# The low halves of the first weight matrix: subtracted by VectorE in place of GpSimd

## Chip, cores and metric

One core of one Trainium2 chip. The metric is the device time of one execution in microseconds (us); smaller is better.

## What is computed

Four batches of eight heads of causal attention with a decay, and behind it two feed-forward blocks over the same 2304 tokens:

```python
scores = where(causal, -1e9, q @ k.T / 8 + cum[:, None] - cum[None, :])   # cum: running sum of log f
attn = softmax(scores); x = attn @ v                   # 4 batches, 8 heads, 576 tokens, 64 wide
h = x @ w_in; g = h * tanh(softplus(h)); z = g @ w_out # 2304 x 512 -> 2048 -> 512
m = maximum(maximum(z @ w1, z @ w2), z @ w3)           # 512 -> 768
out = m @ w_out2                                       # 768 -> 512
```

The weights arrive as 64-bit floats, so the kernel turns them into 32-bit ones itself.

## The kernel before

The matrix products of the feed-forward blocks are made of two halves. An operand t is split by `split` (L129): a high half hi in a shorter format, copied by ScalarE (L131), and a low half lo = t - hi (L137). `mm3` (L179) adds three products into PSUM: high by high (L181), high by low (L182), low by high (L183).

**First stage, where the change lies.** Two streams of work are woven together.

- Attention, sixteen pairs of heads, two units each (`scores`, L338, and `av`, L404). A score product goes to PSUM (L336). VectorE adds the decay and takes the row minimum (L390; tile mn). ScalarE does the exponential and the row sums (L396). VectorE makes the reciprocals rr (L357, L358). GpSimd scales the rows P by rr (L360). TensorE turns P (L429, tile pp), VectorE and ScalarE copy the turned blocks from PSUM into TA and TB (L433, L435), TensorE multiplies by v (L415, tile av), and the result is split into xh (ScalarE, L131) and xl (VectorE, L137). GpSimd also masks the decay tiles cb when they land (L295, L299).
- `h_steps` (L496), the first feed-forward product h = x @ w_in (L181 to L183, tile h), for blocks of 512 tokens as soon as attention has finished them; the results he are copied from PSUM (L522, L519) and sent to DRAM.

`load_w_in` (L198) brings w_in in sixteen pieces of 128 x 512 values: a load by SyncE's queue (L146, tile wr), then `convert` (L151): absolute value by ScalarE (L156), clamp by GpSimd (L160), shift and two merges of the words by VectorE (L163, L166, L170, tile wt), then `split`: high half by ScalarE (L131, tile wi), low half by GpSimd (L137, tile wi). There are two wt buffers, so the absolute value of a piece waits until the subtraction two pieces before has read its buffer.

The order on each engine is made by a scheduler that simulates the program with priorities: attention stands under a high priority (L537), `wgen` (the weight pieces) and the h steps are advanced in between at a fixed rate (L543, L550). An engine works off its instructions strictly in that order.

**Later stages**: h times w_out with the Mish function between, then the three maxima, then the output product. Their code is not touched.

Of the kernel before, what the change touches and what calls it, by code (L numbers as in the profile page):

```python
# [64 lines left out]
def tile_decay_attention__mish_ff__max3_ff(  # L65
# [63 lines left out]
    def split(dst_hi, dst_lo, src, eng_hi, eng_lo):  # L129
        if eng_hi == "act":  # L130
            nc.scalar.activation(dst_hi, src, AF.Copy)  # L131
        elif eng_hi == "pool":
            nc.gpsimd.tensor_scalar(dst_hi, src, 1.0, 1.0, op0=ALU.mult, op1=ALU.mult)
        else:
            nc.vector.tensor_copy(dst_hi, src)
        eng = nc.gpsimd if eng_lo == "pool" else nc.vector
        return eng.tensor_tensor(out=dst_lo, in0=src, in1=dst_hi, op=ALU.subtract)  # L137
# [3 lines left out]
    def fetch(pool, src, bufs):  # L141

        m, n = src.shape[0] // 128, src.shape[1]
        r = pool.tile([128, m, n, 2], I32, name="wr", tag="wr", bufs=bufs)
        with queued(pace):
            nc.sync.dma_start(  # L146
                r.rearrange("p m n w -> p m (n w)"), src.bitcast(I32).rearrange("(m p) w -> p m w", p=128)
            )
        return r

    def convert(pool, r, bufs=None, abs_eng="dve"):  # L151

        t = pool.tile([128, r.shape[1], r.shape[2]], F32, name="wt", tag="wt", bufs=bufs)
        lo, hi, ti = r[:, :, :, 0], r[:, :, :, 1], t.bitcast(I32)
        if abs_eng == "act":
            nc.scalar.activation(t, hi.bitcast(F32), AF.Abs)  # L156
        else:
            nc.vector.tensor_scalar(ti, hi, 0x7FFFFFFF, None, op0=ALU.bitwise_and)
        eng = nc.gpsimd if abs_eng == "act" else nc.vector
        eng.tensor_scalar(  # L160
            t, t, F32_MIN_AS_HIGH_HALF, F32_MAX_AS_HIGH_HALF, op0=ALU.max, op1=ALU.min
        )
        nc.vector.tensor_scalar(  # L163
            ti, ti, 3, 0x3FFFFFF8, op0=ALU.logical_shift_left, op1=ALU.bitwise_and
        )
        nc.vector.scalar_tensor_tensor(  # L166
            out=ti, in0=hi, scalar=-0x40000000, in1=ti,
            op0=ALU.bitwise_and, op1=ALU.bitwise_or,
        )
        nc.vector.scalar_tensor_tensor(  # L170
            out=ti, in0=lo, scalar=29, in1=ti,
            op0=ALU.logical_shift_right, op1=ALU.bitwise_or,
        )
        return t
# [20 lines left out]
    wi = [wpool.tile([128, 2, KD, 256], F32R, name=f"wi{fp}") for fp in range(NFP)]  # L195
    loaded = set()

    def load_w_in():  # L198
        jobs = [(fp, c) for fp in range(NFP) for c in range(0, KD, 2)]
        raws = []  # L200
        for k, (fp, c) in enumerate(jobs):
            for f_, c_ in jobs[len(raws):k + 3]:
                raws.append(fetch(wst, moe_w_in[c_ * 128:(c_ + 2) * 128, f_ * 256:f_ * 256 + 256], 4))
            if k == 0:
                yield
            t = convert(wst, raws[k], abs_eng="act")
            split(wi[fp][:, 0, c:c + 2], wi[fp][:, 1, c:c + 2], t, "act", "pool")
            if c + 2 == KD:
                loaded.add(fp)
            yield  # L210
# [285 lines left out]
    def h_steps():  # L496
# [3 lines left out]
        for i, j in order:  # L500
# [28 lines left out]
            yield i  # L529

    wgen = load_w_in()
    attn = attention()
    steps = h_steps()
# [294 lines left out]
    for t0 in (BLK2, BLK2 + 2 * HALF):  # L828
        hh = [hp2.tile([128, 2 * HALF], F32R, name=f"hh{c}") for c in range(NF2)]
        hl = [hp2.tile([128, 2 * HALF], F32R, name=f"hl{c}") for c in range(NF2)]  # L830
        for p in range(3):
            fs = slice(p * 128, p * 128 + 128)
            for m in range(3):
                S = []
                for k in range(4):
                    t = sst.tile([128, 2, 2, 128], F32R, name="s")
# [88 lines left out]
```

## Time and profile before

| | |
|---|---|
| median of 3 runs | 910.57 us (909.36 to 911.1) |
| the profiled execution | 909.78 us, of it 907.7 us span |
| TensorE (PE) busy | 882.8 us, 97% of the span |
| VectorE (DVE) busy | 497.1 us, 55% |
| ScalarE (ACT) busy | 400.7 us, 44% |
| GpSimd (POOL) busy | 232.7 us, 26% |
| loads and stores | 145.25 MB, mean 160 GB/s |

The span is what the profiler saw between the first and the last instruction; the execution's own time is 2.1 us longer. Shares are means over stages with different limits, so what is to be read is the stage in which the change lies, the first 160 us.

### The profile page before, as it was taken

The numbers are of one execution on the slowest core, as the hardware profiler recorded it, in microseconds if no ns is written. First come the engines' busy times: TensorE is split into PE (matmuls) and PEld (weight loads), VectorE is DVE, ScalarE is ACT, GpSimd is POOL, SyncE is SP. The second block draws the span as 40 slices with busy tenths as digits, with TensorE's granted clock in tenths as the row PEclk, the third lists the DMA queues.
The fourth block names the chain that finished last, engine by engine and source line by source line (L and its number), as shares of the span: only waits on it lengthen the run. The fifth ranks groups of instructions, "written<-read, shape, count | busy, mean of one in ns | idle before, by whom it ended". The sixth has DMA issues, their size and how long they took to land.

```text
span 907.7 us, 13930 instructions
## 1 busy us (share of the span) xinstructions
PE 882.8 (97%) x4800; PEld 704.8 (78%) x4800; DVE 497.1 (55%) x1186; ACT 400.7 (44%) x913; POOL 232.7 (26%) x317
## 2 busy tenths in 40 slices
PE   6898999999999999999999999999999999999998
PEld 3565666767767778889888888889888998889986
DVE  3598675344444343991367575775855447424440
ACT  4687666454443432533465545553433222412211
POOL 3689987222222220000020000000121332013310
PEclk8989999999999999999999999999999999999999
DMA  7896664444333115863456666663499444333401
GB/s 183 227 226 171 179 192 117 115 134 127 105 102 108 47 48 178 292 226 128 143 181 217 214 216 222 217 226 98 162 359 322 124 123 117 111 96 126 139 23 60
DMA packets 125030, 145.25 MB, mean 160 GB/s; under 512 B 64736, under 2 KB 78048, under 8 KB 124960
## 3 DMA queue, kind: packets, MB, share of 16 engines
q1 hardware_dynamic: 105856, 102.41, 39.0%
q10 hardware_dynamic: 16416, 27.79, 8.3%
q0 software_dynamic: 2688, 14.16, 4.3%
q8 instruction: 38, 0.62, 0.3%
q14 instruction: 32, 0.26, 0.1%
HBM read 102.83 MB, written 41.49 MB: 159 GB/s over the span
## 4 chain that ended last, share of the span: by engine, by line
PE 89%; POOL 3%; DMA 2%; DVE 2%; issue 1%; ACT 1%; SPq 1%; POOLq 0%
PE y L181 7%; PE y L183 7%; PE y L182 7%; PE h L181 7%; PE h L182 7%; PE h L183 7%; PE q L182 6%; PE q L183 6%; PE q L181 6%; PE sc L336 5%; PE av L415 5%; PE pp L429 5%; PE o L181 3%; PE o L182 3%; PE o L183 3%; PE g L181 2%
## 5 line engine op out<-in xcount | busy, mean ns | idle before, releaser
L181 PE MATMUL h<-xh,wi 128*128 128x512 f32 (+1 forms) x320 | 121.4, 380 | 1.6 <-ACT he L522 1.3
L182 PE MATMUL h<-xl,wi 128*128 128x512 f32 (+1 forms) x320 | 120.6, 377 | 1.8 <-DVE xl L137 1.8
L183 PE MATMUL h<-xh,wi 128*128 128x512 f32 (+1 forms) x320 | 120.7, 377 | 0.0
L182 PE MATMUL y<-gl,wo 128*128 128x512 f32 (+1 forms) x320 | 117.7, 368 | 0.0
L183 PE MATMUL y<-gh,wo 128*128 128x512 f32 (+1 forms) x320 | 117.6, 368 | 0.0
L181 PE MATMUL y<-gh,wo 128*128 128x512 f32 (+1 forms) x320 | 106.3, 368 | 0.0
L360 POOL TENSOR_SCALAR P<-P,rr 128x128 f32<-128x128 f32 (+3 forms) x128 | 74.0, 592 | 87.5 <-DVE rr L358 31.5
L659 DVE TENSOR_TENSOR gl<-g,gh 128x512 fp32r<-128x512 f32 x72 | 50.0, 697 | 83.3 <-ACT gh L658 83.1
L396 ACT ACTIVATE P<-P,mn 128x128 f32<-128x128 f32 (+3 forms) x128 | 70.7, 554 | 53.4 <-DVE mn L390 50.2
L652 ACT ACTIVATE g<-g 128x512 f32<-128x512 f32 x72 | 45.2, 632 | 70.6 <-DMA g<-h_d 65.7
L181 PEld LDWEIGHTS h<-xh,wi 128*128 128x128 f32 x320 | 60.1, 188 | 14.6 <-issue 2.2
L182 PEld LDWEIGHTS h<-xl,wi 128*128 128x128 f32 x320 | 60.1, 188 | 14.0 <-issue 2.8
L183 PEld LDWEIGHTS h<-xh,wi 128*128 128x128 f32 x320 | 60.3, 188 | 11.5 <-issue 2.7
L182 PEld LDWEIGHTS y<-gl,wo 128*128 128x128 f32 x320 | 60.3, 188 | 10.2
L183 PEld LDWEIGHTS y<-gh,wo 128*128 128x128 f32 x320 | 60.2, 188 | 10.1
L181 PEld LDWEIGHTS y<-gh,wo 128*128 128x128 f32 x320 | 60.3, 189 | 10.1
L522 ACT ACTIVATE he<-h 128x512 f32<-128x512 f32 x56 | 33.3, 595 | 57.0 <-PE h L183 52.4
L851 DVE TENSOR_TENSOR u<-q,p 128x448 f32<-128x448 f32 x36 | 22.4, 621 | 62.3 <-PE q L183 60.7
L336 PE MATMUL sc<-kT,qT 64*128 64x128 f32 (+3 forms) x256 | 51.9, 500 | 3.6 <-DVE mn L390 3.3
L429 PE MATMUL pp<-ident,P 128*128 128x128 f32 x320 | 51.1, 285 | 4.0 <-ACT qT L314 3.6
L658 ACT ACTIVATE gh<-g 128x512 fp32r<-128x512 f32 x72 | 45.0, 627 | 22.0 <-PE y L183 20.9
L429 PEld LDWEIGHTS pp<-ident,P 128*128 128x128 f32 x320 | 37.0, 143 | 20.1 <-issue 5.0
(141 smaller groups left out, 1850.3 us busy)
## 6 DMA issues: line engine op xcount, KB each, us to landing
g<-h_d SPq DMA_DIRECT2D x72, 256.0 KB, 2.9
s<-s_d SPq DMA_DIRECT2D x72, 256.0 KB, 3.0
h_d<-he ACTq DMA_DIRECT2D x56, 256.0 KB, 2.9
wr<-in_moe_w_out_dram SPq DMA_DIRECT2D x22, 512.0 KB, 4.6
wr<-in_moe_w_dram SPq DMA_DIRECT2D x24, 384.0 KB, 3.8
s_d<-sk POOLq DMA_DIRECT2D x12, 768.0 KB, 5.8
cb<-cum_d SPq DMA_DIRECT2D x32, 256.0 KB, 4.2
wr<-in_moe_w_in_dram SPq DMA_DIRECT2D x16, 512.0 KB, 4.5
```

The costliest lines, as they stand in the source:

```text
L181: nc.tensor.matmul(ps, wh, xh, start=start, stop=False, skip_group_check=True)
L182: nc.tensor.matmul(ps, wh, xl, start=False, stop=False, skip_group_check=True)
L183: return nc.tensor.matmul(ps, wl, xh, start=False, stop=stop, skip_group_check=True)
L336: nc.tensor.matmul(dst, lhs, J["k"][rows, c0:c0 + w], start=True, stop=True, skip_group_check=True)
L360: nc.gpsimd.tensor_scalar(made[ci], made[ci], rr[:, ci:ci + 1], 1.0, op0=ALU.mult, op1=ALU.mult)
L396: nc.scalar.activation(Pt, Pt, AF.Exp, scale=-1.0, bias=mn[:, col - 1:col], accum_out=sm[:, ci:ci + 1],)
L415: last = nc.tensor.matmul(acc[(U, L)[h], off:off + w], J["vs"][:, n * 64:n * 64 + 64], T[:, at[h]:at[h] + w], start=kt == 0 and off == 0, ...
L429: turn = nc.tensor.transpose(pp[:, n * 128:n * 128 + 128], Pt[:, k0:k0 + 128], ident)
L522: nc.scalar.activation(he, h, AF.Copy)
L652: nc.scalar.activation(g, g, AF.Mish)
L658: on_act[:] = [nc.scalar.activation(gh, g, AF.Copy)]
L659: on_dve[:] = [nc.vector.tensor_tensor(out=gl, in0=g, in1=gh, op=ALU.subtract)]
```

## The change

One word: the engine of the low half's subtraction of w_in goes from GpSimd to VectorE. The clamp (L160) and the scaling of P (L360) stay on GpSimd. Sixteen subtractions of 128 x 512 values are concerned.

```diff
@@ load_w_in @@
             t = convert(wst, raws[k], abs_eng="act")
-            split(wi[fp][:, 0, c:c + 2], wi[fp][:, 1, c:c + 2], t, "act", "pool")
+            split(wi[fp][:, 0, c:c + 2], wi[fp][:, 1, c:c + 2], t, "act", "dve")
```

The scheduler makes a new order with it on every engine, from about 50 us to the end of attention.

On GpSimd, at the fourth and fifth pieces of w_in, between two scalings of P of one unit (L360). L295 masks the decay tiles of a later pair.

```order
 L360 TENSOR_SCALAR P_0_1143<-P_0_1143,rr 128x384
 L360 TENSOR_SCALAR P_1_1149<-P_1_1149,rr 128x384
-L137 TENSOR_TENSOR wi_149<-wt,wi_149 128x512
-L160 TENSOR_SCALAR wt<-wt 128x512
-L295 AFFINE_SELECT cb<-cb 128x2x256
-L137 TENSOR_TENSOR wi_150<-wt,wi_150 128x512
-L295 AFFINE_SELECT cb<-cb 128x2x128 x2
+L160 TENSOR_SCALAR wt<-wt 128x512
+L295 AFFINE_SELECT cb<-cb 128x2x256
+L295 AFFINE_SELECT cb<-cb 128x2x128 x2
+L160 TENSOR_SCALAR wt<-wt 128x512
 L360 TENSOR_SCALAR P_0_1156<-P_0_1156,rr 128x512
 L360 TENSOR_SCALAR P_1_1162<-P_1_1162,rr 128x512
```

Both subtractions are gone, and the clamp of the next piece has moved up, ahead of the scaling of the wide P.

On VectorE, the place where the second piece is converted, before:

```order
L390 ISA P_None,mn<-sc,cb_602 128x288
L390 ISA mn 128x1
L358 RECIPROCAL rr<-rr 128x2
L390 ISA P_None,mn<-sc,cb_602,mn 128x288
L390 ISA mn 128x1
L163 TENSOR_SCALAR wt<-wt 128x512
L166 SCALAR_TENSOR_TENSOR wt<-wr,wt 128x512
```

and now:

```order
L390 ISA P_None,mn<-sc,cb_602 128x288
L390 ISA mn 128x1
L163 TENSOR_SCALAR wt<-wt 128x512
L137 TENSOR_TENSOR wi_148<-wt,wi_148 128x512
L358 RECIPROCAL rr<-rr 128x2
L390 ISA P_None,mn<-sc,cb_602,mn 128x288
L390 ISA mn 128x1
L166 SCALAR_TENSOR_TENSOR wt<-wr,wt 128x512
```

The shift L163, which waits for GpSimd's clamp, and the moved subtraction, which waits for ScalarE's high half, now stand ahead of a reciprocal and of the second half of a row minimum.

On VectorE again, ahead of the subtraction that gives xl for an h step. Before:

```order
L170 SCALAR_TENSOR_TENSOR wt<-wr,wt 128x512
L390 ISA P_None,mn<-sc,cb_819 128x288
L390 ISA mn 128x1
L137 TENSOR_TENSOR xl_447<-av,xh_446 128x256
L433 COPY TB<-pp 128x512
```

and now:

```order
L390 ISA P_1_1293,mn<-sc,cb 128x256
L390 ISA mn 128x1
L137 TENSOR_TENSOR wi_150<-wt,wi_150 128x512
L163 TENSOR_SCALAR wt<-wt 128x512
L433 COPY TB<-pp 128x512
L137 TENSOR_TENSOR xl_447<-av,xh_446 128x256
```

The same xl comes four row minima later in the order, behind a moved subtraction, a shift and a copy.

## Rows read from the trace of the kernel before

**Rows 1.** The page: busy us (share of span) xinstructions; POOL in 40 slices, tenths.
```profile
PE 882.8 (97%) x4800; PEld 704.8 (78%) x4800; DVE 497.1 (55%) x1186; ACT 400.7 (44%) x913; POOL 232.7 (26%) x317
...
POOL 3689987222222220000020000000121332013310
```

**Rows 2.** Windows: stretch, its length, busy us (xcount) by engine, PEclk, DMA share, GB/s.
```profile
48.00:160.00 112.00, 104.60 (x714) 72.73 (x713) 84.64 (x243) 75.05 (x208) 97.18 (x108) 0.98 0.65 176
60.00:100.00 40.00, 36.50 (x270) 25.53 (x270) 33.26 (x91) 27.81 (x78) 37.55 (x43) 1.00 0.75 195
...
160.00:440.00 280.00, 280.00 (x1712) 214.18 (x1710) 133.91 (x389) 121.95 (x309) 47.64 (x92) 1.00 0.42 133
```

**Rows 3.** Timeline of PE: start, duration, instruction, count [idle before <-releaser].
```profile
45.38 1.11 PE L429 MATMUL pp<-ident,P 128*128 128x128 f32 x4 [3.61 <-ACT qT L314]
...
79.79 0.50 PE L182 MATMUL h<-xl,wi 128*128 128x512 f32 x1 [1.80 <-DVE xl L137]
...
85.13 0.92 PE L336 MATMUL sc<-kT,qT 64*128 64x384 f32 x4 [1.25 <-DVE mn L390]
...
106.83 0.88 PE L336 MATMUL sc<-kT,qT 64*128 64x384 f32 x2 [2.00 <-DVE mn L390]
...
145.97 0.50 PE L181 MATMUL h<-xh,wi 128*128 128x512 f32 x1 [1.32 <-ACT he L522]
```

**Rows 4.** Windows of 2 us behind the long wait; the third number from the end is PEclk.
```profile
46.00:48.00 2.00, 2.00 (x11) 1.03 (x9) 1.82 (x6) 2.00 (x7) 1.91 (x2) 0.50 1.24 226
48.00:50.00 2.00, 2.00 (x12) 1.99 (x11) 2.00 (x9) 1.44 (x6) 0.62 (x2) 0.50 0.83 184
50.00:52.00 2.00, 2.00 (x7) 0.73 (x6) 2.00 (x9) 1.94 (x8) 1.32 (x2) 0.51 1.02 266
```

**Rows 5.** Timeline of DVE at the waits of PE.
```profile
77.31 1.71 DVE L170 SCALAR_TENSOR_TENSOR wt<-wr,wt 128x512 int32<-128x512 int32 x1
...
79.32 0.41 DVE L137 TENSOR_TENSOR xl<-av,xh 128x256 fp32r<-128x256 f32 x1
...
81.99 1.23 DVE L357 TENSOR_SCALAR rr<-sums 128x3 f32<-128x3 f32 x1
...
102.95 0.43 DVE L163 TENSOR_SCALAR wt<-wt 128x512 int32<-128x512 int32 x1 [2.50 <-POOL wt L160]
```

**Rows 6.** Timeline of POOL at the same places.
```profile
77.21 1.26 POOL L137 TENSOR_TENSOR wi<-wt,wi 128x512 fp32r<-128x512 f32 x1
...
81.76 1.43 POOL L137 TENSOR_TENSOR wi<-wt,wi 128x512 fp32r<-128x512 f32 x1
...
98.72 2.30 POOL L295 TENSOR_SCALAR_AFFINE_SELECT cb<-cb 128x512 f32<-128x512 f32 x3 [0.93 <-DMA cb<-cum_d]
101.01 1.91 POOL L160 TENSOR_SCALAR wt<-wt 128x512 f32<-128x512 f32 x1
```

**Rows 7.** Tile wt, 40 to 160 us: duration ns min/median/max, first and last start us.
```profile
L160 POOL TENSOR_SCALAR wt<-wt x16: 1904/1916/2091, 43.2 to 140.2; 128x512 f32<-128x512 f32 x16
L163 DVE TENSOR_SCALAR wt<-wt x16: 417/427/1508, 45.2 to 142.4; 128x512 int32<-128x512 int32 x16
...
L170 DVE SCALAR_TENSOR_TENSOR wt<-wr,wt x16: 678/740/1709, 48.6 to 143.8; 128x512 int32<-128x512 int32 x16
L131 ACT ACTIVATE wi<-wt x16: 615/630/636, 50.0 to 144.8; 128x512 fp32r<-128x512 f32 x16
```

**Rows 8.** Lines of POOL and of DVE, 48 to 160 us: busy, mean | idle before, releasers.
```profile
L137 POOL TENSOR_TENSOR wi<-wt,wi 128x512 fp32r<-128x512 f32 x16 | 22.1, 1391 | 2.1 <-ACT wi L131 2.1
...
L163 DVE TENSOR_SCALAR wt<-wt 128x512 int32<-128x512 int32 x15 | 8.8, 586 | 14.4 <-POOL wt L160 14.4
```

**Rows 9.** Instructions of lines 357, 659 and 137 on DVE: duration ns min/median/max.
```profile
L357 DVE TENSOR_SCALAR rr<-sums x64: 147/170/1374, 17.0 to 337.6; 128x2 f32<-128x2 f32 x48, 128x3 f32<-128x3 f32 x16
...
L659 DVE TENSOR_TENSOR gl<-g,gh x72: 678/693/953, 423.3 to 622.4; 128x512 fp32r<-128x512 f32 x72
...
L137 DVE TENSOR_TENSOR xl<-av,xh x48: 197/380/426, 28.7 to 356.0; 128x256 fp32r<-128x256 f32 x24, 128x64 fp32r<-128x64 f32 x8, 128x192 fp32r<-128x192 f32 x8, 128x128 fp32r<-128x128 f32 x8
```

**Rows 10.** Timeline of ACT ahead of the last wait of PE.
```profile
144.80 0.63 ACT L131 ACTIVATE wi<-wt 128x512 fp32r<-128x512 f32 x1 [1.63 <-DVE wt L170]
```

## The prediction

> **What bounds the kernel now.** I read the page first: TensorE is busy for 97% of the span, GpSimd for 26%, but its slices show it at nine tenths only between the third and the seventh, that is up to about 160 us [rows 1]. So the share of the whole says nothing, and I went to the windows. From 160 to 440 us TensorE is busy in 280.00 of 280 us: nothing that another engine does there could make it faster, and a time saved or lost earlier is passed on to the end unchanged. From 48 to 160 us TensorE is busy in 104.60 of 112 us, GpSimd in 97.18, VectorE in 84.64 [rows 2]. All sixteen moved subtractions lie in this stretch. **What the change can give is therefore at most the 7.4 us that TensorE stands idle there** (112 - 104.60), and the question is which of it hangs on GpSimd.
>
> Then the timeline of TensorE. Four waits make 6.37 us of the 7.4: 1.80 us for an xl, 1.25 and 2.00 us for row minima, 1.32 us for ScalarE's copy he [rows 3]. A fifth, 3.61 us at 45.38 us, comes ahead of the first moved instruction and stays as it is; so does the half clock that follows it, 0.50 in the three windows from 46 to 52 us [rows 3, 4].
>
> Then the engines that were waited for. Ahead of the xl at 79.32 us VectorE's merge L170 took 1.71 us, where its shortest takes 0.68; it began at 77.31, a tenth of a us after GpSimd's subtraction at 77.21, which ran until 78.47. Ahead of the row minima at 84 us the little L357 took 1.23 us instead of 0.15; it began at 81.99, and GpSimd's subtraction of 81.76 ran until 83.19 [rows 5, 6, 7, 9]. In both, VectorE's instruction ends its usual length after GpSimd's subtraction has ended: it was **held**. Five such holds by a subtraction of w_in stand in the timeline (the others at 69, 127 and 134 us), about 1.05 us each. The xl subtraction, which reads PSUM and one tile of SBUF, shows none of it: 0.38 us in the median, 0.43 at the longest [rows 9].
>
> The Trainium skill has the reason on its page "SBUF — State Buffer", section "Who interferes with whom": VectorE and GpSimd share one pair of SBUF ports, taken as a lock for a whole instruction, by any GpSimd operation and by VectorE's two-port modes or operations with two SBUF inputs. The rows agree (held from start to end, 1.71 against 0.68 us). The rule also speaks against this change, since the moved subtraction has two SBUF inputs wherever it runs; that is the third rival below.
>
> **The change, part by part.** The sum is made against the profiled execution, 909.78 us, which lies 0.79 us under the median of 910.57; I add that at the end.
>
> 1. *Removed from GpSimd*: 16 subtractions, 22.1 us in the stretch [rows 8]. GpSimd goes from 97.18 to about 75.1 of 112 us, from 87% to 67%. It stops being the fullest engine after TensorE.
> 2. *The hold ahead of the xl*: 1.71 - 0.68 = 1.03 us of the 1.80 us wait goes. The rest of that wait (0.77) is the merge and the row minimum that stand ahead of xl, and they remain.
> 3. *The hold ahead of the row minima*: 1.23 - 0.15 = 1.08 of 1.25 us goes.
> 4. *The 2.00 us wait at 106.83*: VectorE stood 2.50 us for a clamp [rows 5], and that clamp stood in GpSimd's queue behind masks, which had themselves waited 0.93 us for a load [rows 6]. So the subtractions are only part of the lateness. Bounds 0 and 2.00; nothing divides it better, so I take the middle, 1.0.
> 5. *The 1.32 us wait at 145.97*: ScalarE stood 1.63 us for a merge of w_in, with he queued behind its high half [rows 10]; the merge was late because its clamp was. Bounds 0 and 1.32; I take the middle, 0.66.
> 6. *Added to VectorE*: 16 subtractions. The nearest row is gl, the same shape and formats on this engine: 0.69 us, up to 0.95 [rows 9]. 16 x 0.69 = 11.0 us; the five holds give back 5 x 1.05 = 5.3. VectorE goes from 84.64 to about 90.4 of 112 us, 81%. I cost it at nothing on the path: VectorE stands 14.4 us waiting for clamps in this stretch [rows 8], and an emptier GpSimd makes those earlier, so the new work fills idle time. If that cover is gone the price is that of the first rival.
> 7. *New waits*: the subtraction waits on VectorE for ScalarE's high half, and the order puts row minima, reciprocals (which GpSimd's scaling waits for) and the xl behind it. On GpSimd the same wait cost 2.1 us in all [rows 8]; below lies nothing, and above all sixteen times a whole high half, 16 x 0.63 = 10.1 us [rows 7]. The order leaves other work between a piece's last merge and its subtraction, so I stay with the nearest row, 0 to 2.1, on an engine with slack: nothing on the path.
> 8. *A new order on TensorE*: the kinds of product change 378 times in the old order and 375 times in the new. No term.
> 9. *Loads*: the same loads in a new order on SyncE's queue; TensorE waited for none in this stretch. No term.
>
> Sum: 1.03 + 1.08 + 1.0 + 0.66 = 3.77 us less. 909.78 - 3.8 = 906.0, and with 0.79 for the median **906.8 us**. What is late next is VectorE itself, which then carries more than GpSimd.
>
> **The rivals.** A measurement of this kernel tells a change from none at about 0.2%, 1.8 us.
>
> - *VectorE fills up (slower).* From 60 to 100 us VectorE is busy in 33.26 of 40 us [rows 2], and some 6.4 of the sixteen pieces fall there (16 x 40/100). Its idle 6.74 us pay 1.05 us for each: **over 1.05 us per subtraction, held time and waits for ScalarE included, VectorE becomes the bound**. A subtraction that meets a clamp in the middle takes 0.69 + 1.92/2 = 1.65 us; 6.4 x 1.65 = 10.6, or 3.8 us too much, which TensorE loses behind xl and the row minima. 909.78 + 3.8 + 0.79 = 914.4 us. For it: shifts and merges of w_in already stretch to 1.5 and 1.7 us [rows 7], and the order puts the shift, which waits for the clamp, ahead of a row minimum. Against it: half of what stretches them disappears, and 14.4 us of waiting for the clamp is there to be used. One more wait of TensorE as long as 3.61 us could also bring a second stretch at half clock, some 3 us more [rows 3, 4]. Chance 0.20.
> - *The order swallows it (no change).* The scheduler made a different order on every engine for 100 us; other places become late in place of these, as the xl that now stands behind a moved subtraction. Then 910.6 us. Nothing in the profile speaks for it except that each of the four waits is under 2 us and has its own cause. Chance 0.10.
> - *The hold changes sides (no change).* The subtraction is held by clamps and holds GpSimd in turn; its 11.0 us take the place of 22.1, so half of the holds come back. Terms 4 and 5 then give nothing, 2 and 3 give half: 2.11/2 = 1.06, and 910.57 - 1.06 = 909.5 us. For it: L170, the merge with the same two SBUF inputs, was held for 1.03 us by GpSimd. Against it: on VectorE the subtraction is half as long as on GpSimd (0.69 against 1.39 us), so it is in the way for a shorter time. By the Trainium skill's section named above the port lock would do exactly this. Chance 0.15.
>
> **How the numbers follow.** Forecast, faster by over 0.2%: 0.55. No change, the second and third rival: 0.25. Slower: 0.20. The best case is that all 7.4 us of idle time go: 909.78 - 7.4 + 0.79 = 903.2 us, the low end. The high end is the price of the first rival, 914.4 us; beyond it lies about half of that rival's 0.20 (several subtractions held for a whole clamp, or a second stretch at half clock), so some 0.1 is left out there and little below. The forecast's own range is 903.2 to 908.7.
>
> **What would show it.** Right: in the same stretch (up to 160 us) GpSimd falls by about 22 us of busy time, VectorE rises by 5 to 7, TensorE's idle time behind 48 us falls from 7.4 to about 3.6; the sixteen subtractions of wi stand on VectorE with a median near 0.7 us; L357 and L163 have few instructions over 1 us; VectorE's wait for the clamp falls well under 14.4 us; from 160 us on nothing differs but a shift. Wrong: a median of the wi subtraction over 1.05 us, new waits of TensorE for xl or mn of 2 us and more, or a TensorE clock under 1.00 between 60 and 160 us.

## The result, and the profile after

| | before | after |
|---|---|---|
| median of 5 runs | 910.46 us (909.36 to 911.1) | **915.59 us** (915.05 to 919.91) |
| the profiled execution | 909.78 us, span 907.7 | 915.05 us, span 913.2 |

The ratio is 1.0072, with a 95% interval of 1.0046 to 1.0098: slower by 0.7%, where 906.8 us was forecast.

The page of the changed kernel: busy time by engine, and GpSimd's slices.

```profile
PE 885.9 (97%) x4800; PEld 707.8 (78%) x4800; DVE 499.7 (55%) x1202; ACT 401.4 (44%) x913; POOL 214.4 (23%) x301
...
POOL 3689763222222220000010000000121323013310
```

And the windows of the same three stretches.

```profile
48.00:160.00 112.00, 101.68 (x668) 68.21 (x666) 85.07 (x255) 73.20 (x200) 78.50 (x91) 0.97 0.60 167
60.00:100.00 40.00, 34.73 (x249) 22.75 (x247) 35.66 (x108) 29.71 (x84) 35.63 (x39) 0.96 0.70 190
160.00:440.00 280.00, 279.73 (x1728) 216.00 (x1728) 134.28 (x390) 121.72 (x310) 47.80 (x92) 1.00 0.43 134
```

Beside [rows 2]: from 48 to 160 us GpSimd fell by 18.7 us (97.18 to 78.50) and VectorE rose by 0.4, although it has sixteen subtractions more (over the whole span by 2.6, 497.1 to 499.7; at 160 us the changed kernel is behind and has done less of its other work). So the work went where it was meant to go, and yet TensorE's idle time in the stretch rose from 7.4 to 10.3 us. From 160 to 440 us TensorE is full, as before.

The span grew by 5.5 us: 2.4 are more idle time of TensorE (24.9 to 27.3 over the whole span), 3.1 more busy time for the same 4800 products. Most of both comes from two places of the stretch. The timeline of TensorE there:

```profile
80.70 0.55 PE L429 MATMUL pp<-ident,P_None 128*128 128x128 f32 x3 [1.88 <-DVE TB L433]
82.53 0.99 PE L429 MATMUL pp<-ident,P 128*128 128x128 f32 x4 [1.29 <-ACT TB L435]
...
126.10 0.50 PE L181 MATMUL h<-xh,wi 128*128 128x512 f32 x1 [2.94 <-ACT he L522]
```

None of the four waits of [rows 3] is left; these three stand ahead of other products. Behind each of the two places the granted clock fell from 1.00 (2.4 GHz) to 0.50 (1.2 GHz) for some 3.4 us. Windows of 2 us, PEclk third from the end:

```profile
82.00:84.00 2.00, 1.47 (x6) 1.13 (x8) 2.00 (x7) 2.00 (x9) 2.00 (x3) 0.66 0.71 218
84.00:86.00 2.00, 2.00 (x6) 0.72 (x3) 2.00 (x8) 1.45 (x5) 1.91 (x4) 0.50 0.81 199
126.00:128.00 2.00, 1.90 (x7) 1.42 (x8) 1.87 (x6) 1.67 (x6) 1.55 (x3) 0.76 0.71 246
128.00:130.00 2.00, 2.00 (x8) 1.36 (x7) 1.94 (x4) 1.79 (x5) 2.00 (x2) 0.50 0.77 187
130.00:132.00 2.00, 2.00 (x9) 1.08 (x8) 0.74 (x1) 0.79 (x2) 1.91 (x3) 0.89 0.20 71
```

A window at share c does (1 - c) of its length less work, so by this estimate the two spells cost 1.7 us each. The first spell, at 46 us, was shorter in this execution (0.78, 0.50 and 0.87 from 44 to 50 us) than in the one of before [rows 4], which gives 1.7 back. Of the 3.1 us more busy time that leaves 1.4 that I can't place.

What was late at these places stands on VectorE:

```profile
77.48 0.84 DVE L163 TENSOR_SCALAR wt<-wt 128x512 int32<-128x512 int32 x1 [1.37 <-POOL wt L160]
78.25 0.90 DVE L137 TENSOR_TENSOR wi<-wt,wi 128x512 fp32r<-128x512 f32 x1
79.07 0.90 DVE L166 SCALAR_TENSOR_TENSOR wt<-wr,wt 128x512 int32<-128x512 int32 x1
...
79.97 0.68 DVE L433 COPY TB<-pp 128x512 f32<-128x512 f32 x1
...
123.54 0.62 DVE L163 TENSOR_SCALAR wt<-wt 128x512 int32<-128x512 int32 x1 [2.67 <-POOL wt L160]
124.09 0.50 DVE L390 CUSTOM_DVE_ANT_0 P_None<-sc,cb,mn 128x288 f32<-128x288 f32 x1
```

Both times the shift L163 stands at VectorE's head and waits for GpSimd's clamp, 1.37 and 2.67 us, and what TensorE needs is queued behind it: at 79.97 the copy TB, at 124.09 the second half of a row minimum. Ahead of the copy the moved subtraction itself adds 0.90 us. The second one goes on through ScalarE, where the exponential waited 3.48 us for that minimum, with the copy he of the h step behind it:

```profile
124.70 0.78 ACT L396 ACTIVATE P_None<-P_None,mn 128x576 f32<-128x576 f32 x1 [3.48 <-DVE mn L390]
...
125.47 0.58 ACT L522 ACTIVATE he<-h 128x512 f32<-128x512 f32 x1
```

The moved operation itself did what was forecast. The steps of one piece (tile wt), with durations in ns min/median/max:

```profile
L160 POOL TENSOR_SCALAR wt<-wt x16: 1907/1917/2234, 43.1 to 130.6; 128x512 f32<-128x512 f32 x16
L163 DVE TENSOR_SCALAR wt<-wt x16: 398/427/843, 45.0 to 132.9; 128x512 int32<-128x512 int32 x16
...
L170 DVE SCALAR_TENSOR_TENSOR wt<-wr,wt x16: 667/692/1085, 48.1 to 134.5; 128x512 int32<-128x512 int32 x16
...
L137 DVE TENSOR_TENSOR wi<-wt,wi x16: 672/716/1037, 52.0 to 136.9; 128x512 fp32r<-128x512 f32 x16
```

Against [rows 7] the longest shift fell from 1508 to 843 ns and the longest merge from 1709 to 1085: the holds by GpSimd's subtraction are gone. In return some of GpSimd's instructions are held by the moved subtraction. What is left on GpSimd took 3.4 us more than before (78.50 against 97.18 - 22.1 = 75.1), and the longest scaling of P rose from 1.17 to 1.64 us; it began while a subtraction ran on VectorE:

```profile
127.00 1.02 DVE L137 TENSOR_TENSOR wi<-wt,wi 128x512 fp32r<-128x512 f32 x1
...
127.47 1.64 POOL L360 TENSOR_SCALAR P<-P,rr 128x512 f32<-128x512 f32 x1
```

The last clamp starts at 130.6 us instead of 140.2: the pieces come earlier, and TensorE gained nothing by it.

So two things changed at once, the engine of an operation and the scheduler's order on all engines. The experiments take them apart.

### The profile page after: what moved, and what is told of

Same layout as the page of the kernel before. It is cut to its first block, busy times and chain, and to the rows that moved or that the text cites. A ratio compares the mean times of both kernels' runs of the same rounds, so it can differ in the third digit from the quotient of the medians.

```text
span 913.2 us, 13993 instructions
## 1 busy us (share of the span) xinstructions
PE 885.9 (97%) x4800; PEld 707.8 (78%) x4800; DVE 499.7 (55%) x1202; ACT 401.4 (44%) x913; POOL 214.4 (23%) x301
## 4 chain that ended last, share of the span: by engine, by line
PE 87%; DVE 4%; DMA 3%; POOL 2%; issue 1%; ACT 1%; SPq 1%; POOLq 0%; ACTq 0%
PE y L181 7%; PE y L183 7%; PE y L182 7%; PE h L181 7%; PE h L183 6%; PE h L182 6%; PE q L182 6%; PE q L181 6%; PE q L183 6%; PE sc L336 5%; PE pp L429 5%; PE av L415 4%; PE o L181 3%; PE o L182 3%; PE o L183 3%; PE g L181 2%
## 5 line engine op out<-in xcount | busy, mean ns | idle before, releaser
L360 POOL TENSOR_SCALAR P<-P,rr 128x128 f32<-128x128 f32 (+3 forms) x128 | 75.3, 603 | 102.6 <-DVE rr L358 59.2
L658 ACT ACTIVATE gh<-g 128x512 fp32r<-128x512 f32 x72 | 44.9, 626 | 19.6 <-PE y L183 18.7
```

The source lines that it names most:

```text
L360: nc.gpsimd.tensor_scalar(made[ci], made[ci], rr[:, ci:ci + 1], 1.0, op0=ALU.mult, op1=ALU.mult)
L658: on_act[:] = [nc.scalar.activation(gh, g, AF.Copy)]
```

## The experiments

Where an order is "held", a table of instruction numbers gives each engine's order in the first stage, and a call at the kernel's end adds an order-only dependency between neighbours on each engine. In the traces of runs 1, 2, 4, 7 and 11 every instruction that was not moved stands in the order of the table from the first piece on. No run holds an order without any other edit, so what the call costs by itself is not measured. The call:

```diff
         tile_decay_attention__mish_ff__max3_ff(tc, *args)
+        pinned(nc, tc)
```

All results, each with its own ratio to the kernel before on the same chip (median of before 909.7 to 910.5 us):

| run | subtraction, clamp | order | median us | ratio (95%) |
|---|---|---|---|---|
| 1 | DVE, POOL | before's, held | 907.42 | 0.9972 (0.9962 to 0.9983) |
| 2 | POOL, POOL | changed one's, held | 929.54 | 1.0207 (1.0192 to 1.0222) |
| 3 | DVE, POOL | changed one's, three moved | 917.67 | 1.0086 (1.0066 to 1.0105) |
| 4 | DVE, DVE | changed one's, held | 906.54 | 0.9965 (0.9952 to 0.9978) |
| 5 | DVE, POOL | pieces later | 910.26 | 1.0009 (0.9995 to 1.0023) |
| 6 | DVE, POOL | pieces earlier | 913.67 | 1.0044 (1.0030 to 1.0059) |
| 7 | DVE, DVE | before's, held | **901.37** | 0.9910 (0.9897 to 0.9924) |
| 8 | DVE, DVE | its own | 905.90 | 0.9964 (0.9951 to 0.9977) |
| 9 | DVE, DVE | pieces earlier | 910.56 | 1.0004 (0.9994 to 1.0014) |
| 10 | DVE, DVE | pieces later | 909.18 | 0.9989 (0.9978 to 0.9999) |
| 11 | POOL, DVE | before's, held | 903.15 | 0.9916 (0.9902 to 0.9929) |
| 12 | POOL, DVE | its own | 915.52 | 1.0062 (1.0048 to 1.0075) |
| 13 | POOL, POOL | another from 89 us on (rate 0.98) | 912.72 | 1.0033 (1.0021 to 1.0045) |
| 14 | POOL, POOL | before's again (rate 1.05) | 909.73 | 0.9998 (0.9989 to 1.0007) |
| 15 | DVE, POOL | changed one's again to 361 us (rate 0.98) | 921.50 | 1.0110 (1.0083 to 1.0137) |
| 16 | DVE, POOL | changed one's again to 180 us (rate 1.05) | 919.39 | 1.0092 (1.0074 to 1.0110) |

**Runs 1 and 2: the engine and the order apart.** My theory: the loss is the order's. The rival: VectorE with the subtractions is what makes TensorE wait.

Run 1 is the changed kernel with the table of before's order (the subtractions stand where the scheduler likes them); run 2 the kernel before with the table of the changed order.

> The sixteen subtractions run on VectorE as in the change, but every other instruction of every engine is held to the order of the kernel before by edges between neighbours; only where on VectorE the subtractions stand is left to the scheduler. Theory 1, the loss comes from the new order (VectorE stands in its queue for GpSimd's clamp ahead of attention's work, and two waits of TensorE of about 3 us end in a stretch at half clock): the loss goes away, 906 to 911 us, with no half clock between 60 and 160 us and TensorE idle for under 7.4 us from 48 to 160. Theory 2, the loss is the 11 us of work that VectorE has more: still 914 us or more.

> The counterpart: the sixteen subtractions stay on GpSimd as in the kernel before, but every other instruction is held to the order that the scheduler made for the change. Theory 1 (order): as slow as the change or slower, 915 to 922 us, since the clamps come later still behind the subtractions. Theory 2 (VectorE's load): back near 910.5 us.

Run 1, the window of 48 to 160 us:

```profile
48.00:160.00 112.00, 106.86 (x728) 74.68 (x727) 84.70 (x261) 77.00 (x215) 79.00 (x92) 0.98 0.65 176
```

Run 1 took 907.42 us, under both kernels. VectorE and GpSimd are as busy as in the changed kernel (84.70 and 79.00 against 85.07 and 78.50), and TensorE stands idle for 5.1 us where it stood for 10.3. **The move of the subtraction alone gives about 2.5 us; the new order costs some 8** (915.59 against 907.42). Against the expectation one spell at half clock is left between 60 and 160 us, 0.57 in the two windows from 106 to 110. Run 2 says the same from the other side: without the move, the new order costs 19 us, more than the 915 to 922 us that I had expected. There GpSimd has the subtractions again, and through the two wt buffers ScalarE waits for them, from 40 to 160 us:

```profile
ACT wt L156 <- POOL wi L137: 35.9, 12, 5.3
```

(us in total, times, longest). The absolute value of a piece waits for a free buffer with exponentials queued behind it. What is left in run 1 above 1 us is one wait; timelines of TensorE, VectorE and GpSimd:

```profile
104.27 0.88 PE L336 MATMUL sc<-kT,qT 64*128 64x384 f32 x2 [2.44 <-DVE mn L390]
```

```profile
99.83 0.43 DVE L163 TENSOR_SCALAR wt<-wt 128x512 int32<-128x512 int32 x1 [3.85 <-POOL wt L160]
```

```profile
95.84 0.64 POOL L295 TENSOR_SCALAR_AFFINE_SELECT cb<-cb 128x512 f32<-128x512 f32 x1 [3.24 <-DMA cb<-cum_d]
...
97.88 1.92 POOL L160 TENSOR_SCALAR wt<-wt 128x512 f32<-128x512 f32 x1
```

The clamp stands in GpSimd's queue behind masks that wait for a load. It is the wait of 2.00 us in [rows 3], with the same cause as in [rows 6], not shortened by the move.

**Run 3: is it the three places?** The changed order with three instructions moved: on VectorE the copy TB ahead of the shift L163, and the second half of a row minimum ahead of the later L163; on ScalarE another TB ahead of an absolute value L156. The two on VectorE:

```diff
+L433 COPY TB<-pp 128x512
 L163 TENSOR_SCALAR wt<-wt 128x512
 L137 TENSOR_TENSOR wi_150<-wt,wi_150 128x512
 L166 SCALAR_TENSOR_TENSOR wt<-wr,wt 128x512
 L357 TENSOR_SCALAR rr<-sums_172 128x3
-L433 COPY TB<-pp 128x512
...
-L163 TENSOR_SCALAR wt<-wt 128x512
 L390 ISA P_None,mn<-sc,cb_1238,mn 128x288
 L390 ISA mn 128x1
+L163 TENSOR_SCALAR wt<-wt 128x512
```

> The changed kernel with its own order held, but for three instructions: on VectorE the copy TB that TensorE waited for at 80.7 us is put ahead of the shift that waits for a clamp; on ScalarE the copy TB that it waited for at 82.5 us is put ahead of an absolute value; on VectorE the second half of the row minimum is put ahead of the shift that stood 2.67 us for a clamp, which made TensorE wait 2.94 us at 126.1. Theory 1 (these waits, and the half clock behind them): most of 1.88 + 1.29 + 2.94 = 6.1 us of waits goes and so do the two stretches of 3.4 us at half clock, in all 5 to 8 us less, 907.5 to 911 us. Theory 2 (load): the waits turn up elsewhere, 914 us or more.

The first theory fell: 917.67 us. The three waits went and two others came, for a row minimum (2.7 us) and for a copy by ScalarE (2.9 us). From TensorE's waits from 40 to 160 us, in total, times, longest:

```profile
PE sc L336 <- DVE mn L390: 4.1, 4, 2.7
...
PE pp L429 <- ACT q L317: 2.9, 1, 2.9
```

Each was again followed by a spell at half clock (84 to 88 and 128 to 136 us). I read the three places as symptoms: with them mended, TensorE waits elsewhere in the same order.

**Runs 4, 7, 8, 11, 12: the clamp.** The clamp goes to VectorE too, so that no step of VectorE waits for GpSimd in the middle of a piece; in runs 11 and 12 it goes alone.

```diff
-        eng = nc.gpsimd if abs_eng == "act" else nc.vector
+        eng = nc.vector
```

> The changed kernel in its own order, but the sixteen clamps also run on VectorE (0.36 to 0.42 us each, 6 to 7 us more work there, about 31 us less on GpSimd). Where they stand on VectorE is left to the scheduler. Theory 1, VectorE stands 13.6 us for clamps that are late on GpSimd and that is what makes TensorE wait: those waits go to zero, 906 to 912 us although VectorE works more. Theory 2, VectorE has too much work: slower than the change, 917 us or more.

> The subtraction and the clamp on VectorE, everything else in the order of before. If waiting for GpSimd's clamp is what is left of TensorE's waits (2.44 us for a row minimum and the half clock behind it in the run with the old order): 903.5 to 905.5 us, TensorE busy in over 108 of 112 us from 48 to 160 us. If VectorE's own load (then some 90 of 112 us) is what is left: 906 to 908 us, as with the clamp on GpSimd. Between this and the run with the clamp on VectorE in the changed order (906.54 us) stands what the two orders cost when nothing waits for GpSimd: nothing, if the order hurts only through the clamp; up to 8 us, if it hurts by itself.

> The subtraction and the clamp on VectorE, in the order that the scheduler makes for that, with nothing held fixed. If a fresh order costs only where pieces wait for GpSimd in between: 904 to 908 us. If each fresh order is a draw, good or bad by some us: anything from 904 to 916 us, and outside 904 to 908 it speaks for the draw.

> The kernel before, in its own order held fixed, with the clamp alone moved to VectorE; the subtraction stays on GpSimd. If the two moves add up: before 909.7, less the 6.0 us that the clamp's move gave behind the subtraction's (907.42 to 901.37): 903.7 us. If GpSimd's subtractions still hold VectorE's merges and make TensorE wait for xl and row minima: 906 to 909 us, with L170 or L357 over 1.2 us at the longest.

> The same edit in the order that the scheduler makes for it, nothing held. If a fresh order costs some us wherever it comes from: 906 to 914 us, over the run with the order fixed by 2 us or more. If it does so only where VectorE waits for GpSimd's clamp: as the run with the order fixed, within 2 us.

In the changed order the clamp's move brings 9 us (915.59 to 906.54), in before's order 6 behind the subtraction's (907.42 to 901.37, 2 us better than the most I had expected) and 7 alone. Windows of runs 4, 7, 11 and 12, in this order:

```profile
48.00:160.00 112.00, 107.61 (x720) 72.54 (x717) 88.96 (x278) 77.70 (x216) 53.27 (x78) 0.98 0.63 173
60.00:100.00 40.00, 36.65 (x252) 23.93 (x253) 39.14 (x123) 31.29 (x88) 24.98 (x36) 0.96 0.79 212
```

```profile
48.00:160.00 112.00, 110.14 (x759) 77.02 (x758) 93.40 (x281) 80.31 (x222) 51.51 (x78) 1.00 0.68 182
60.00:100.00 40.00, 38.89 (x287) 27.21 (x286) 38.51 (x114) 29.11 (x81) 21.78 (x32) 1.00 0.81 212
```

```profile
48.00:160.00 112.00, 110.20 (x742) 76.55 (x743) 89.76 (x264) 79.03 (x218) 68.32 (x94) 0.98 0.68 181
```

```profile
48.00:160.00 112.00, 98.72 (x665) 67.10 (x665) 85.16 (x252) 73.22 (x199) 67.81 (x92) 0.96 0.60 166
```

VectorE is busy for 39.14 and 38.51 of 40 us in runs 4 and 7, far more than in the changed kernel (35.66), and both are faster: a full VectorE is not the bound. What fits all these runs is a VectorE that *stands* ahead of attention's work. In run 7 no wait of TensorE in the stretch is longer than 0.8 us, and its median is the lowest of all, 0.9% under the kernel before; run 11, whose interval overlaps with its own, is not clearly behind. Run 8, both moves in a fresh order, took 905.90 us, 4.5 more than run 7; that lies inside both of its ranges and decides nothing.

Run 11 has the subtraction on GpSimd, and the holds with it:

```profile
L170 DVE SCALAR_TENSOR_TENSOR wt<-wr,wt x16: 680/872/1656, 48.4 to 136.9; 128x512 int32<-128x512 int32 x16
```

The longest merge still takes 1.66 us, and no wait for xl or a row minimum is among TensorE's from 40 to 160 us (of my rival there came the holds, not the time). So in before's order, with the clamp gone from GpSimd, the holds cost TensorE nothing. That they made it wait in [rows 3] because waits for the clamp had used up the slack is my reading; no run shows it by itself.

Runs 11 and 12 are the same edit in two orders, 903.15 and 915.52 us, 12 us apart, more than any engine move here is worth (what this one brings in before's order is 7). In run 12 the shift no longer waits for a clamp, yet TensorE waits 10.7 us for row minima (six times, longest 4.7), because the chain now goes through the buffers:

```profile
ACT wt L156 <- POOL wi L137: 12.3, 8, 2.9
```

```profile
92.57 0.46 DVE L160 TENSOR_SCALAR wt<-wt 128x512 f32<-128x512 f32 x1 [1.78 <-ACT wt L156]
...
94.66 0.68 DVE L390 CUSTOM_DVE_ANT_1 P<-sc,cb 128x512 f32<-128x512 f32 x1
```

It is the same figure with another instruction in it: a step of w_in stands ahead of a row minimum and waits. That a fresh order costs only where VectorE waits for GpSimd's clamp falls with run 12, which is also 1.5 us slower than the other range that I had given.

**Runs 5, 6, 9, 10: the places of the pieces.** The order is cut in two: the 128 instructions of w_in's pieces, and all others. Runs 5 and 10 take the others from the changed order and the pieces' places from before's, runs 6 and 9 the reverse, held by the same call. Places don't carry over exactly, and both overshoot: shifts stand behind 58.7 row minima in the mean (5, 10) and 53.0 (6, 9).

> The subtraction on VectorE. Attention and the h steps stand in the changed kernel's order among themselves; the sixteen pieces of w_in (loads, absolute value, clamp, shift, merges, halves) are put back to where the order of before has them, by the count of other instructions ahead of them in the whole program, which puts the sixteen shifts 58.7 row minima from the start in the mean (changed kernel 55.0, before 56.8). If the changed kernel is slow because its pieces stand too early, ahead of clamps that are not ready (my theory now): 906 to 909 us, no half clock between 60 and 160 us. If the order of attention itself is the worse one: 914 to 917 us, as the changed kernel, with waits for sc or pp of 2 us and more in about the same places.

> The counterpart. The subtraction on VectorE, attention and the h steps in the order of before, the pieces of w_in put to where the changed kernel has them, by the same count; that makes them stand earlier still (53.0 row minima ahead of a shift in the mean, against 55.0). If pieces that stand too early are the cause: 914 to 920 us, with VectorE's wait for the clamp over 13.6 us and a half clock between 60 and 160 us. If the order of attention is the cause: 906 to 909 us, as with everything in the order of before (907.4).

> As the run with the pieces earlier in the order of before (913.67 us), and the clamp on VectorE too. If pieces that stand too early hurt only because VectorE then waits for GpSimd's clamp: 901 to 903 us, as with the pieces in their old places (901.37). If they hurt by themselves (ScalarE's halves and absolute values and VectorE's work ahead of attention): 905 to 910 us, with waits of TensorE for xh, xl or mn of over 1 us between 60 and 110 us.

> As the run with the pieces later in the changed kernel's attention order (910.26 us), and the clamp on VectorE too. The changed order with the clamp on VectorE took 906.54 us, the order of before 901.37: of these 5.2 us either the places of the pieces are the cause, then this takes 901 to 903.5 us, or attention's own order, then 905 to 907 us.

With the clamp on GpSimd the four corners are 907.42 (both from before), 913.67 (pieces earlier), 910.26 (attention from the changed one) and 915.59 us (both). By these medians the places of the pieces carry 5.3 to 6.3 us of the 8.2, attention's own order 1.9 to 2.8. Runs 5 and 6 lie between the two ranges given for each, and the changed order itself took up to 921.50 us in runs 15 and 16 below, so the sizes, and which of the two carries more, are not settled. The expected side effect did not come: in run 6 VectorE waits only 4.8 us for the clamp, but 5.5 us in nine waits for the high half wi; which link of a piece is the late one changes with the order. With the clamp on VectorE the corners are 901.37, 910.56, 909.18 and 906.54: earlier pieces cost 9.2 us in before's order and nothing in the changed one (906.54 against 909.18). Run 10 is slower than either of its ranges. "Too early" is therefore no property of the pieces alone, and that pieces hurt only through the clamp is refuted by run 9.

**Runs 13 to 16: other orders of both kernels?** Only the rate at which h steps are advanced is changed, which was to make the scheduler order all engines anew.

```diff
-        credit += RATE
+        credit += 0.98 * RATE
```

> The kernel before; only the rate at which h steps are advanced beside attention is 0.98 of what it was, which makes the scheduler draw another order on every engine and moves no work between engines. If before's order is not special: 909 to 911.5 us. If it is a good draw among many: slower by 3 us or more, 913 to 922 us.

> The same with the rate at 1.05, whose order is nearer to that of before. Not special: 909 to 911.5 us; a good draw: 912 us or more.

> The changed kernel (subtraction on VectorE), with the rate at 0.98. If the loss belongs to the move: 914 to 917 us, as the changed kernel. If the order is a draw: anywhere from 905 to 925 us, and a difference of over 3 us from 915.6 speaks for the draw.

> The changed kernel with the rate at 1.05. If the loss belongs to the move: 914 to 917 us. If the order is a draw: anywhere from 905 to 925 us, and a difference of over 3 us from 915.6 speaks for the draw.

Three of the four are no other orders. In the trace of run 14 every engine has the same instructions in the same sequence as in the kernel before, to the end. In runs 15 and 16 every engine has the changed kernel's sequence up to 361 and 180 us, so in the whole stretch, and TensorE waits in the same places, as its waits of run 15 show:

```profile
PE h L181 <- ACT he L522: 3.6, 1, 3.6
PE pp L429 <- DVE TB L433: 1.9, 1, 1.9
```

So these three are repeats. Run 14 repeats the kernel before within 0.1%. Runs 15 and 16 repeat the loss, and with the same order in the stretch they are 3.8 to 5.9 us slower than the changed kernel (run 15 alone spans 914.15 to 923.15 us). Part of that is the clock: 0.94 from 48 to 160 us in both against 0.97. My bound for a draw, over 3 us from 915.6, was passed without another order and so shows no draw; nor does run 3, 2.1 us over the changed kernel in nearly the same order, differ from it clearly.

Only run 13 is another order: 912.72 us, 2.2 more than the kernel before, between its two ranges. Of the subtraction alone on VectorE no second order of the stretch was measured, so whether the scheduler's orders for this edit are all bad stays open. What is shown is that the loss is not in the engine move, which gains in before's order.

## Why the prediction was wrong

- **Terms 1 and 6 held in the main.** GpSimd fell by 18.7 us (22.1 forecast), since 3.4 us came back as holds on its other instructions. VectorE rose by 0.4 (5 to 7 forecast), since more was given back than the five holds of 1.05 us and less other work falls into the stretch. By lines, 48 to 160 us, busy us and mean ns behind the bar:

```profile
L137 DVE TENSOR_TENSOR wi<-wt,wi 128x512 fp32r<-128x512 f32 x16 | 12.6, 789 | 0.9 <-ACT wi L131 0.7
L170 DVE SCALAR_TENSOR_TENSOR wt<-wr,wt 128x512 int32<-128x512 int32 x16 | 12.3, 768 | 0.1
L163 DVE TENSOR_SCALAR wt<-wt 128x512 int32<-128x512 int32 x15 | 7.4, 492 | 12.9 <-POOL wt L160 12.9
...
L357 DVE TENSOR_SCALAR rr<-sums 128x2 f32<-128x2 f32 (+1 forms) x23 | 5.5, 245 | 1.3 <-ACT P_None L396 1.0
```

  And before, beside the 8.8 us of L163 in [rows 8]:

```profile
L170 DVE SCALAR_TENSOR_TENSOR wt<-wr,wt 128x512 int32<-128x512 int32 x16 | 14.4, 897 | 0.2
...
L357 DVE TENSOR_SCALAR rr<-sums 128x2 f32<-128x2 f32 (+1 forms) x23 | 11.2, 487 | 1.0 <-ACT P_None L396 0.5 <-ACT P L396 0.4
```

  For the three together that is 9.2 us less now, against 12.6 us of subtractions. VectorE's wait for the clamp, in the third row, fell only from 14.4 to 12.9 us; that it would fall "well under" was wrong.
- **Terms 2 to 5, the gain of 3.77 us, came about to two thirds, and only in the order of before**: run 1 took 2.5 us less than the kernel before. There the waits for the row minima at 85 us and for he at 146 us are gone, the same xl comes 0.6 us late (another 0.9), and term 4, where I took the middle of 0 and 2.00, was worth nothing: 2.44 us instead of 2.00, masks and a load being its cause. Wait by wait this proves little: in run 14, which repeats the kernel before, the waits of 1.25 and 1.32 us are missing too, without any move.
- **The step that failed is the pricing of the order**, at three points. Term 7 said of the shift and subtraction placed ahead of row minima "on an engine with slack: nothing on the path"; term 8 counted kinds of product on TensorE and set "No term"; and the rival "The order swallows it" was given 910.6 us and a chance of 0.10, with "Nothing in the profile speaks for it except that each of the four waits is under 2 us and has its own cause". Measured, the order costs 8.2 us (run 1 against the changed kernel), twice the gain and more; two spells at half clock are part of it. The profile did speak for it: VectorE's 14.4 us of waits for clamps [rows 8] are slack only as long as nothing stands behind them in its queue. I counted that time as cover for new work; it is the price list for every place where attention's work moves behind a waiting step.
- **The rivals.** "VectorE fills up" came near the time (914.4) by another mechanism: its point was 1.05 us per subtraction, the median is 0.72, and runs 4 and 7 are faster with a fuller VectorE, so that the time came near was luck. One of its arguments does name what happened: the shift, which waits for the clamp, ahead of a row minimum. Its side remark on a second stretch at half clock came true, twice, behind waits shorter than it asked for. "The hold changes sides" occurred in part: 3.4 us more on GpSimd's other instructions, a scaling of P of 1.64 us, clamps of up to 2.23 us, at an unchanged median of the clamp (1917 ns against 1916). In run 1 the same holds stand (longest clamp 2.46 us) and the kernel gains, so they are not the loss. By the Trainium skill's page "SBUF — State Buffer", section "Who interferes with whom", whoever has the shared ports blocks the other for a whole instruction; the rows agree where VectorE is the one held (1656 ns against 680 for a merge in run 11) and where GpSimd is (1.64 us for the scaling at 127.47 us).
- **Signs named beforehand.** A TensorE clock under 1.00 between 60 and 160 us was named as what would show the forecast wrong, and it stood there; but run 14, which repeats the kernel before, has it too (78 to 84 and 106 to 114 us), so the sign doesn't tell the two kernels apart. New waits for xl or row minima of 2 us and more did not come: the new wait of 2.94 us is for he, which stood behind a late row minimum on ScalarE.

**What stays open:** which property makes an order good. By the medians the places of the pieces carry most of the difference while the clamp is on GpSimd, but no count that I made (row minima ahead of a shift) ranks all orders: run 8, at 53.0, takes 905.9 us, run 9, with the same mean of 53.0, 910.6. A third wt buffer, which would loosen the chain of run 12, was not tried.

## What to carry to other kernels

Where a scheduler makes the order, moving an operation to another engine is two changes; hold the old order and time the move by itself, since here the moves gave 2.5 to 8 us in the old order and new orders took 4.5 to 12 back. A small edit meant to draw a new order may not draw one: three of four here repeated the old. On an engine that works strictly in order, waiting time is slack only if nothing urgent is queued behind the waiting instruction: before costing new work at nothing, look at what stands behind each such wait in the *new* order. And take away the step that makes a chain cross to a slow engine (here the clamp, 1.92 us against 0.43 on VectorE) before the one that merely loads that engine.

## What was not expected of the hardware

- **The clock fell to half behind waits much shorter than the 3.61 us that I had reckoned with** [rows 3, 4]: 2.94 us in the changed kernel and, close together, 1.88 and 1.29; 2.44 in run 1, 1.80 and 1.68 in run 14, 1.11 in run 4. The length of a wait doesn't decide: the kernel before has run 14's order and waits of 1.80 and 2.00 us, and the clock stayed at 1.00 behind both. In run 8 it did so behind 3.08 us. What decides, no run here shows. Runs 14 and 8, waits and windows behind them:

```profile
78.81 0.50 PE L182 MATMUL h<-xl,wi 128*128 128x512 f32 x1 [1.80 <-DVE xl L137]
...
80.00:82.00 2.00, 2.00 (x10) 1.47 (x10) 1.76 (x2) 0.69 (x2) 2.00 (x3) 0.50 0.80 287
```

```profile
105.89 1.03 PE L336 MATMUL sc<-kT,qT 64*128 64x384 f32 x2 [1.68 <-DVE mn L390]
...
108.00:110.00 2.00, 2.00 (x8) 1.06 (x7) 1.23 (x6) 0.99 (x2) 1.92 (x5) 0.50 0.41 93
```

```profile
44.69 0.66 PE L429 MATMUL pp<-ident,P 128*128 128x128 f32 x4 [3.08 <-ACT qT L314]
...
46.00:48.00 2.00, 1.35 (x11) 0.93 (x10) 2.00 (x6) 1.98 (x7) 0.33 (x1) 1.00 1.03 191
```

- **The clamp takes 0.43 us on VectorE and 1.92 on GpSimd**, for the same 128 x 512 values and formats; the subtraction 0.72 and 1.28 (medians). The clamp, which the change left on GpSimd, gains far more by such a move than the subtraction that it moved.
